# Half-folded mixer rows for batch 0, and a third head pair of q on the hardware queue

## The chip, the cores and the metric

The kernel runs on one core of a Trainium2 chip. The metric is the device time of one execution in microseconds (us). A core has five engines that work side by side: TensorE (PE, matmuls; PEld is its weight load), VectorE (DVE), ScalarE (ACT), GpSimd (POOL) and SyncE (SP, which here only starts DMAs). TensorE writes its results to PSUM, a memory of eight banks; VectorE and ScalarE copy them out.

## The reference

Eight batches; attention over keys and values that are averaged over groups of 8 tokens, then a mixer over tokens and over channels:

```
k_p = k.reshape(B, H, Sp, 8, D).mean(axis=3)      # B=8, H=8, S=576, D=64, Sp=72
v_p = v.reshape(B, H, Sp, 8, D).mean(axis=3)
x   = softmax(q @ k_p^T / sqrt(D)) @ v_p          # then heads side by side: (B, 576, 512)
u   = x + (relu(x^T @ w_tok1) @ w_tok2)^T         # w_tok1 576 x 256, w_tok2 256 x 576
out = u + relu(u @ w_ch1) @ w_ch2                 # w_ch1 512 x 1536, w_ch2 1536 x 512
```

Inputs and outputs are fp32; the kernel multiplies in bf16.

## The kernel before

**Units and batches.** The mixer's channel part is done in nine units (`unit_steps`, L546): unit n takes the first 512 tokens of batch n, and a last unit takes the 64 remaining tokens of all eight batches. A unit first makes the 1536 hidden channels as 12 blocks m of 128: four matmuls of 512 columns each over the transposed rows `uT` (L553), and a relu on ScalarE into `GT` (L557). Then it makes the output, 12 matmuls for each block c of 128 tokens (L575), and `store` adds u on VectorE (L561) and writes it out by SP. The generator yields after every two matmuls of 512 columns, so a full unit has 48 steps.

**The order of work.** Every engine has one queue of instructions, and its order is written out by hand in strings. `HEAD` (L597) lists the steps of batch 0 before unit 0. `FIRST`, `SECOND`, `THIRD`, `FOURTH` and `LATER` (L600 to L617) give, for units 0, 1, 2, 3 and all later ones, what is put in at which of the unit's steps: a plain name is a step of batch n+1, `>` one of batch n+2, `<` one of batch n itself, and `lk2` starts the load of k for batch n+2.

**Names of steps.** `K0 K1 V0 V1` average half the heads of k or v on GpSimd (`pool8`, L141; three additions), `k0 v0 v1` the same on VectorE, `kpool vpool` on TensorE (L224). `kpT` (L193) transposes the averaged k; it needs both of `K0` and `K1`. `Q0` to `Q3` transpose q on VectorE (L246). `s0 s1 s2` make scores and their exp on ScalarE (L258 and L263, L276 and L297). `av0` to `av4` (L378) multiply by v and divide; `at0 at1` (L429) are the first token matmul with its relu into `AT`; `u0` to `u4` (L440, L449) the second, with x added; `t0` to `t4` (L458) transpose u into `uT`. From batch 3 on this goes through DRAM instead (`M`, `T`).

**Batch 0 in the head.** `c0 c1` cast the first two head pairs of q, which SP loads as fp32 into `qf` (L648); the other two pairs come through GpSimd's queue with a cast in the DMA (`load_q`, L102). On GpSimd's queue they stand after k and ahead of v. `kp0` to `kp3` average k of one pair on TensorE (L202) with a cast into `kpz` by VectorE, by ScalarE for kp1 (L205); `kt` transposes (L213) and VectorE copies to `kT` (L216). `q0` to `q3` transpose q (L237). `e`, `o` (L313) and `z` (L333) are scores with exp. `w30A` is `half_av` (L341) of token block 3 and head half 0: matmuls (L350), a reciprocal, and the division on VectorE (D) or as four scaled copies on ScalarE (A); a trailing t or p names another PSUM pool. `g`, `h` (L410) are parts of the token matmul, half 0 and half 1, a third digit choosing one m. `d8` are matmuls that only keep TensorE busy.

**The folded rows.** For batch 0, `uT` isn't transposed from u. `X0` to `X3` (L491) put the transposed x into four PSUM banks, one for each part kk, by multiplying with the identity, and `A0 A1` (L499) add the second token matmul to the same banks, transposed by exchanging its operands. Four casts (L502), two on VectorE, two on ScalarE, write `uT`. u itself is still needed for the store, and is made in unit 0 (`<u0` to `<u3`).

**Buffers.** PSUM's eight banks are three of `ps_one` (one bank each, taken in turn), two of `ps_two` (two banks each) and one of `ps_tr`. A step that takes a bank waits until the reader of the use before is done.

Of the kernel before, what the change touches and what calls it, by code (L numbers as in the profile page):

```python
# [8 lines left out]
FP32 = mybir.dt.float32  # L9
# [12 lines left out]
def kernel(  # L22
# [14 lines left out]
    nc = tc.nc  # L37
# [30 lines left out]
    w_ch1 = singles.tile([P, 4, DC], BF16)  # L68
    w_ch2 = singles.tile([P, NM, DM], BF16)
    f2 = singles.tile([P, 2, S], BF16)  # L70
    qf = singles.tile([P, 2, BR * D], FP32)
    kpz = singles.tile([SP, H, 4, D], BF16)
    uT_tails = singles.tile([P, 4, 4 * P], BF16)
    u_tails = singles.tile([P, 4, DM], BF16)
# [23 lines left out]
    def load_q(b):  # L98
        qb = loaded[b, "q"] = raw.tile([P, HP, BR * D + D], BF16, name="qb")
        if b == 0:  # L100
            nc.vector.memset(qb[:, :, BR * D:], 0.0)
            nc.gpsimd.dma_start(out=qb[:, 2:HP, 0:BR * D], in_=q_pairs(2, HP))  # L102
        else:
            nc.gpsimd.dma_start(out=quarters(qb), in_=q[b].rearrange("(g l) (j n) d -> (l j) g (n d)", l=4, n=2 * BR))  # L104

# [48 lines left out]
    def batch_steps(b):  # L154
# [297 lines left out]
        def uT(c):  # L452
            def go():
                src = st["u"][:, c, :] if c < 4 else u_tails[:, b // 2, :]
                dst, o = (late("uT"), c * P) if c < 4 else (uT_tails, b // 2 * P)
                ps = ps_tr.tile([P, 4, P], BF16, name="pt")
                for kk in range(4):
                    nc.tensor.transpose(out=ps[:, kk, :], in_=parts(src)[:, kk], identity=ident)  # L458
                nc.vector.tensor_copy(out=dst[:, :, o:o + P], in_=ps)
            return go  # L460

        def spill(i):
# [18 lines left out]
                                    in_=st["v"][:, 4 * c:4 * c + 4, :].rearrange("t a (f k) -> t a k f", k=4))  # L481
            return go

        def uT_x(kk, c0, c1):

            def go():
                if c0 == 0:
                    st["uT_ps", kk] = (ps_one.tile([P, 512], FP32, name="p1") if kk < 3 else
                                       ps_two.tile([P, 2, 512], FP32, name="p2")[:, 0])
                for c in range(c0, c1):  # L490
                    nc.tensor.matmul(out=st["uT_ps", kk][:, c * P:(c + 1) * P],  # L491
                                     lhsT=parts(st["x"][:, c, :])[:, kk], rhs=ident, start=(c == 0), stop=False)
            return go

        def uT_a(m):
            def go():
                for kk in range(4):
                    ps = st["uT_ps", kk]
                    nc.tensor.matmul(out=ps, lhsT=parts(st["AT"][:, m, :])[:, kk], rhs=w_tok2[:, m, 0:512],  # L499
                                     start=False, stop=(m == 1))  # L500
                    if m == 1:
                        (nc.scalar.copy if kk % 2 else nc.vector.tensor_copy)(out=late("uT")[:, kk, :], in_=ps)  # L502
            return go

        name = {"kpT": kpT}
# [24 lines left out]
        for c in range(5):  # L530
            for a in range(2):
                for e in "DA":
                    for bank in ("", "t", "p"):
                        name[f"w{c}{a}{e}{bank}"] = half_av(c, a, e, bank)
        for kk in range(4):
            name[f"X{kk}"] = uT_x(kk, 0, 4)
        name["A0"], name["A1"] = uT_a(0), uT_a(1)
        name["Xa"], name["Xb"] = uT_x(0, 0, 2), uT_x(0, 2, 4)
        for i in range(3):
            name[f"M{2 * i}"] = spill(i)  # L540
        name["M"] = quads
# [4 lines left out]
    def unit_steps(n, st):  # L546

        GT = gtp.tile([P, NM, 4 * P], BF16, name="GT")
        uT = uT_tails if n == B else st["uT"]
        for m in range(NM):  # L550
            ps = ps_one.tile([P, 512], FP32, name="p1")
            for kk in range(4):
                nc.tensor.matmul(out=ps, lhsT=w_ch1[:, kk, m * P:(m + 1) * P], rhs=uT[:, kk, :],  # L553
                                 start=(kk == 0), stop=(kk == 3))
                if kk == 1:
                    yield
            nc.scalar.activation(out=GT[:, m, :], in_=ps, func=AF.Relu)  # L557
            yield
        def store(c, ps):
            o_sb = outp.tile([P, DM], FP32, name="o")  # L560
            nc.vector.tensor_tensor(out=o_sb, in0=ps, in1=(u_tails if n == B else st["u"])[:, c, :], op=ALU.add)  # L561
            for half in range(2):
                b, r = (2 * c + half, 8) if n == B else (n, 2 * c + half)
                nc.sync.dma_start(out=out[b].rearrange("(p r) n -> p r n", r=BR)[:, r, :],
                                  in_=o_sb[half * BP:(half + 1) * BP, :])

        runs = [(c, 0, NM) for c in range(3 if n == B else 4)]
        if n == 0:
            runs[0:2] = [(c, m, m + 4) for m in (0, 4, 8) for c in range(2)]
        pss = {}  # L570
        for c, m0, m1 in runs:
            if m0 == 0:
                pss[c] = ps_one.tile([P, 512], FP32, name="p1")
            for m in range(m0, m1):
                nc.tensor.matmul(out=pss[c], lhsT=GT[:, m, c * P:(c + 1) * P], rhs=w_ch2[:, m, :],  # L575
                                 start=(m == 0), stop=(m == NM - 1))
                if m == NM - 1:
                    store(c, pss[c])
                if m % 2 == 1:
                    yield  # L580
        if n < B:
            return
        for a in range(2):
            cols = slice(a * 256, (a + 1) * 256)
            ps = ps_one.tile([P, 512], FP32, name="p1")
            for m in range(NM):
                nc.tensor.matmul(out=ps[:, 0:256], lhsT=GT[:, m, 3 * P:4 * P], rhs=w_ch2[:, m, cols],  # L587
                                 start=(m == 0), stop=(m == NM - 1))
            o_sb = outp.tile([P, DM], FP32, name="o")[:, 0:256]
            nc.vector.tensor_tensor(out=o_sb, in0=ps[:, 0:256], in1=u_tails[:, 3, cols], op=ALU.add)  # L590
            for half in range(2):
                (nc.scalar if half else nc.sync).dma_start(
                    out=out[6 + half].rearrange("(p r) n -> p r n", r=BR)[:, 8, cols],
                    in_=o_sb[half * BP:(half + 1) * BP, :])


    HEAD = """c0 c1 d8 q0 d1 q1 d5 kp0 kp1 kt0 kp2 e0 o0 kt1 kp3 kt2 o1 q3 q2 e1 kt3 vpool0 z2 z0 w30A w10Dt  # L597
              w00D z1 w20Dt vpool1 w40Dt g21 w11D w21Dp g20 g11 g40 g31 g10 w01D g30 g00 w31D h1 w41Dp g41 h0 h2
              h3 g01 X1 h4 X2 Xa X3 Xb A0 A1"""
    FIRST = {0: "<u1 <u3", 1: "<u2 <u0 k0 lv2", 3: "Q0 Q1", 4: "lk3", 6: "lq3 Q2", 7: "Q3", 10: "kpool1 v0",  # L600
             11: "lv3", 12: "kpT", 14: "s0", 15: "v1", 19: "s1", 25: "s2", 26: "av0", 27: "av1", 29: ">K1 av2",
             30: "av4", 31: "av3", 33: "at1", 34: "at0", 35: ">K0", 36: ">V1 u0", 37: "u2 u1", 38: ">V0", 39: "t0",
             41: "t1 u4 u3", 42: "t2", 44: "t3", 46: "t4"}
    SECOND = {0: "lq3 Q0 kpT", 1: "Q1 lv3 Q2", 2: ">K1", 3: "s0", 4: ">V0", 6: "Q3", 7: ">K0 lk3", 8: "s1 >V1",
              13: "s2", 16: "av0 av1", 19: "av2", 20: "av3", 22: "av4", 23: "at0", 24: "at1 >Q0", 26: "u0", 27: "u1",
              29: "t0", 31: "u2 t1", 32: "u3 t2", 34: "t3", 35: "lq4", 36: ">kpT >Q1", 37: ">Q2 lv4", 39: ">s0",
              43: ">Q3", 44: ">s1", 47: "lk4"}
    THIRD = {0: "av1 >V0", 1: ">K1", 3: ">K0", 4: "av0", 6: "av3", 7: "av2", 9: "av4", 10: ">Q0 >V1 at0", 11: "at1",
             14: "u0", 15: "u2 u1", 17: "u3 M0 M2", 18: "u4 M4", 19: ">Q1", 24: "M", 26: ">Q3 >kpT", 28: ">s0 lq4",
             29: ">Q2", 32: ">s1 lk4", 33: "T0", 34: "lv4", 36: "T1 T2", 38: ">av0", 39: ">av2", 41: ">av1 T3",  # L610
             45: ">av3", 46: ">av4", 47: "T4"}
    FOURTH = {1: ">V0 M4 u4 at0 at1", 2: ">K0", 3: "u0", 4: "u1", 5: ">K1", 7: "u2", 9: "u3 M0", 10: "M2 >V1",
              11: "M", 14: ">Q1", 20: "lq4 >kpT", 21: "lv4", 22: ">Q0", 23: ">Q2", 24: "T0 lk4", 26: ">s0", 28: ">Q3",
              29: "T1", 32: "T2 >s1", 35: "T3", 36: "T4", 39: ">av0", 41: ">av1", 43: ">av2", 46: ">av4 >av3"}
    LATER = {0: ">V0", 1: "at1 at0", 2: ">V1", 3: "u0 >K0 u1", 5: "u2 u4", 9: "M4 >K1", 11: "M0 u3", 12: "M2",
             14: "M", 18: ">Q1 >kpT", 19: ">Q0", 21: ">s0", 24: ">Q3", 27: ">Q2", 28: ">s1", 29: "T0 T1", 30: "T2",
             34: "T3", 35: ">av1", 38: ">av0", 39: "T4", 41: ">av2", 46: ">av4 >av3"}  # L617
    warm = singles.tile([P, 512], BF16)

    def head(s):  # L620
# [23 lines left out]
    with tc.manual_schedule(engines={PE, POOLE, DVE, ACT, SYNC}):  # L644
        batches = [batch_steps(b) for b in range(B)]
        nc.vector.memset(warm, 0.0)
        for a in range(2):
            nc.sync.dma_start(out=qf[:, a:a + 1, :], in_=q_pairs(a, a + 1))  # L648
        load("k", 0)
        make_identity(nc, ident)  # L650
# [53 lines left out]
```

The softmax here doesn't subtract the row's maximum and nothing guards it: scores larger than these inputs give would overflow.

## Time and profile before

| what | us |
|---|---|
| median of 8 runs | 273.78 (273.32 to 274.53) |
| the profiled execution | 273.53 |
| its span, first to last instruction | 271.8 |
| idle of TensorE's weight loads for k, at 6.92 | 0.88 |
| the same for v, at 12.05 | 0.79 |
| first matmul of unit 0 | at 22.76 |
| first hidden matmul of unit 1 | at 55.96 |

Durations of single operations before:

| operation | ns |
|---|---|
| relu into GT, ScalarE, 128x512 (L557) | 598 |
| cast into uT, 128x512: VectorE, ScalarE (L502) | 685, 588 |
| u plus x, VectorE, 128x512 (L449) | 688 |
| fp32 q cast, 128x576: ScalarE, VectorE (L627) | 672, 460 |
| averaging half of k or v on GpSimd (L144, L145, L148 or L150) | 2120, 1264, about 720 |

The page of the profile lists groups of instructions by line; an engine's idle time ahead of a group is given with what ended it. The answers in order of time give start, duration, engine, line and operation. Matmuls overlap: the distance between two starts is the cost in a stream[...].

### The profile page before, as it was taken

The page shows a single profiled execution, that of the slowest core. Times are in us where ns is not written, and L with a number is a line of the kernel's source. Part 1 is how long each engine was busy: PE and PEld are TensorE (multiplying, and loading weights), DVE is VectorE, ACT ScalarE, POOL GpSimd, SP SyncE. Part 2 cuts the span into 40 slices and gives each one's busy share as a digit, 9 for nine tenths or more (in the row PEclk, how much of TensorE's full clock was granted, in tenths as well). Part 3 has the DMA queues.
Part 4 walks back from the last instruction along what each step waited for, and adds up shares of the span by engine and source line. Part 5 has one row for each costly group of instructions (what it writes and reads, how often), then busy time and mean ns, then how long its engine had stood idle before and what let it go on. Part 6 is the DMA issues. An engine that isn't in the chain of part 4 may idle for free.

```text
span 271.8 us, 4534 instructions
## 1 busy us (share of the span) xinstructions
PE 264.4 (97%) x1812; PEld 129.3 (48%) x1812; DVE 142.0 (52%) x279; ACT 110.9 (41%) x192; POOL 130.5 (48%) x119
## 2 busy tenths in 40 slices
PE   7899999999999999999999999999999999999994
PEld 3774444444454544544444445544454444444443
DVE  4587777862684754776366537743773161022022
ACT  2443780058206536325732483158304503603700
POOL 8694222999995994999199999300000000000000
PEclk9999999999999999999999999999999999999999
DMA  8999999995548957994399372224133544024024
GB/s 170 184 202 208 203 205 206 222 200 93 88 72 154 212 107 154 150 221 125 80 165 212 99 136 59 69 67 118 42 78 92 119 75 102 1 61 94 2 52 103
DMA packets 40149, 33.99 MB, mean 125 GB/s; under 512 B 16960, under 2 KB 33600, under 8 KB 40128
## 3 DMA queue, kind: packets, MB, share of 16 engines
q0 software_dynamic: 18672, 17.64, 41.0%
q1 hardware_dynamic: 21296, 15.93, 23.4%
q8 instruction: 14, 0.23, 0.4%
q10 hardware_dynamic: 160, 0.13, 0.2%
q14 instruction: 7, 0.06, 0.1%
HBM read 38.86 MB, written 12.45 MB: 189 GB/s over the span
## 4 chain that ended last, share of the span: by engine, by line
PE 89%; ACT 3%; DMA 2%; DVE 2%; POOL 1%; issue 1%; POOLq 0%
PE p L553 33%; PE p L575 32%; PE p L429 6%; PE p L440 5%; PE p L378 3%; DMA vr<-in_v_dram 2%; PE p L276 2%; ACT ex L263 1%; ACT GT L557 1%; PE p L224 1%; PE p L587 1%; PE pt L276 1%; PE p L446 1%; PE pt L458 1%; ACT ex L297 1%
## 5 line engine op out<-in xcount | busy, mean ns | idle before, releaser
L557 ACT ACTIVATE GT<-p 128x512 bf16<-128x512 f32 x108 | 63.9, 598 | 90.5 <-PE p L553 90.2
L575 PE MATMUL p<-w_ch,GT 128*128 128x512 bf16 x420 | 100.1, 379 | 0.0
L553 PE MATMUL p<-uT,w_ch 128*128 128x512 bf16 x384 | 91.8, 379 | 0.1
L553 PEld LDWEIGHTS <-w_ch 128*128 128x128 bf16 x432 | 40.5, 98 | 48.2 <-issue 3.1
L575 PEld LDWEIGHTS <-GT 128*128 128x128 bf16 x420 | 38.4, 98 | 40.4
L561 DVE TENSOR_TENSOR o<-p,u 128x512 f32<-128x512 f32 x32 | 21.9, 685 | 52.0 <-PE p L575 52.0
L449 DVE TENSOR_TENSOR u<-p,x 128x512 bf16<-128x512 f32 x32 | 21.5, 688 | 18.8 <-PE p L440 18.4
L145 POOL TENSOR_TENSOR t<-t 72x512 f32<-72x512 f32 x24 | 30.3, 1264 | 1.9
L144 POOL TENSOR_TENSOR t<-kr 72x1024 f32<-72x1024 bf16 x12 | 25.4, 2120 | 7.9 <-DMA kr<-in_k_dram 7.1
L144 POOL TENSOR_TENSOR t<-vr 72x1024 f32<-72x1024 bf16 x12 | 25.5, 2126 | 0.7
L297 ACT ACTIVATE ex<-p 72x1024 bf16<-72x1024 f32 x20 | 19.3, 1015 | 8.9 <-PE p L276 8.9
L246 DVE STREAM_TRANSPOSE qD<-qb 128x576 bf16<-128x576 bf16 x28 | 20.6, 795 | 0.4 <-DMA qb<-in_q_dram 0.4
L396 DVE TENSOR_TENSOR x<-p,den 128x512 bf16<-128x512 f32 x28 | 19.4, 692 | 1.0
L440 PE MATMUL p<-AT,w_tok 128*128 128x512 bf16 x64 | 18.2, 379 | 0.2 <-ACT GT L557 0.2
L378 PEld LDWEIGHTS <-ex 72*128 72x128 bf16 x280 | 13.1, 98 | 8.0 <-DVE x L396 0.6
L480 DVE STREAM_TRANSPOSE uT<-v 128x512 bf16<-128x512 bf16 x20 | 12.9, 686 | 6.0 <-DMA v<-mem 5.9
L429 PE MATMUL p<-x,w_tok 128*128 128x512 bf16 x56 | 14.5, 379 | 0.0
L378 PE MATMUL p<-vp,ex 72*128 72x65 bf16 x280 | 14.3, 194 | 0.2 <-ACT ex L263 0.2
L390 DVE RECIPROCAL den<-p 128x8 f32<-128x8 f32 (+1 forms) x35 | 7.0, 200 | 12.5 <-PE p L378 12.2
L104 POOL DMA_DIRECT2D qb<-in_q_dram x7 | 5.2, 738 | 16.8 <-DVE qD L246 13.0
L429 PEld LDWEIGHTS <-w_tok 128*128 128x128 bf16 x70 | 6.8, 98 | 8.4 <-issue 0.3
L86 POOL DMA_DIRECT2D vr<-in_v_dram x10 | 7.7, 774 | 6.1 <-DMA kr<-in_k_dram 3.1
(109 smaller groups left out, 218.4 us busy)
## 6 DMA issues: line engine op xcount, KB each, us to landing
out_dram<-o SPq DMA_DIRECT2D x70, 128.0 KB, 2.4
kr<-in_k_dram POOLq DMA_DIRECT2D x7, 576.0 KB, 12.9
qb<-in_q_dram POOLq DMA_DIRECT2D x7, 576.0 KB, 6.7
vr<-in_v_dram POOLq DMA_DIRECT2D x7, 576.0 KB, 14.9
w_ch<-in_moe_w_ch_dram POOLq DMA_DIRECT2D x6, 512.0 KB, 13.4
mem<-u SPq DMA_DIRECT2D x10, 256.0 KB, 2.1
v<-mem SPq DMA_DIRECT2D x12, 160.0 KB, 3.6
v<-mem SPq DMA_DIRECT2D x8, 128.0 KB, 3.3
```

Source lines behind the costliest of these rows:

```text
L144: eng.tensor_tensor(out=t4[:, 0:n], in0=t[:, hs, 0:4], in1=t[:, hs, 4:8], op=ALU.add)
L145: eng.tensor_tensor(out=t4[:, 0:n, 0:2], in0=t4[:, 0:n, 0:2], in1=t4[:, 0:n, 2:4], op=ALU.add)
L246: nc.vector.transpose(out=late("qD")[:, g, db].rearrange("m (r j u) -> m u r j", u=2, r=BR), in_=st["qraw"][:, g].rearrange("m (u r d) -> ...
L297: nc.scalar.activation(out=exv[:, a, :, 0:8 * BP], in_=main[a][0:SP], func=AF.Exp, scale=scale)
L378: nc.tensor.matmul(out=halves[h // 4][:, (h % 4) * (D + 1):(h % 4 + 1) * (D + 1)], lhsT=st["ex"][:, h * S + n0:h * S + n0 + P], rhs=st["vp ...
L429: nc.tensor.matmul(out=ps, lhsT=w_tok1[:, c if c < 4 else 4 + par, m * P:(m + 1) * P], rhs=st["x"][:, c, :] if c < 4 else st["xt"], start= ...
L440: nc.tensor.matmul(out=ps, lhsT=w_tok2[:, m, c * P:(c + 1) * P], rhs=st["AT"][:, m, :], start=(m == 0), stop=(m == 1))
L449: nc.vector.tensor_tensor(out=dst, in0=ps, in1=x, op=ALU.add)
L553: nc.tensor.matmul(out=ps, lhsT=w_ch1[:, kk, m * P:(m + 1) * P], rhs=uT[:, kk, :], start=(kk == 0), stop=(kk == 3))
L557: nc.scalar.activation(out=GT[:, m, :], in_=ps, func=AF.Relu)
L561: nc.vector.tensor_tensor(out=o_sb, in0=ps, in1=(u_tails if n == B else st["u"])[:, c, :], op=ALU.add)
L575: nc.tensor.matmul(out=pss[c], lhsT=GT[:, m, c * P:(c + 1) * P], rhs=w_ch2[:, m, :], start=(m == 0), stop=(m == NM - 1))
```

## The change

For batch 0, only the first 256 tokens of `uT` are folded. `X0` and `X1` now take two parts kk each, with two token blocks; `A0` and `A1` multiply by 256 columns. Two casts instead of four remain, of the same size. The other 256 tokens are transposed from u, as in later batches: `u2` and `u3` move to the end of the head, `t2` and `t3` into unit 0's first steps, with the copy on ScalarE and `t3` in a `ps_one` bank. So that unit 0 can begin with the first 256 tokens, its first four hidden blocks are made in two halves of 256 tokens (`hidden`); the number of steps stays the same.

The third head pair of q moves from GpSimd's queue to SP's, as fp32, with the cast `c2` on ScalarE. All six order strings differ.

```diff
-    qf = singles.tile([P, 2, BR * D], FP32)
+    qf = singles.tile([P, 3, BR * D], FP32)
...
-            nc.gpsimd.dma_start(out=qb[:, 2:HP, 0:BR * D], in_=q_pairs(2, HP))
+            nc.gpsimd.dma_start(out=qb[:, 3:HP, 0:BR * D], in_=q_pairs(3, HP))
...
-                ps = ps_tr.tile([P, 4, P], BF16, name="pt")
+                odd = first and c % 2
+                ps = (ps_one if odd else ps_tr).tile([P, 4, P], BF16, name="p1" if odd else "pt")
                 for kk in range(4):
                     nc.tensor.transpose(out=ps[:, kk, :], in_=parts(src)[:, kk], identity=ident)
-                nc.vector.tensor_copy(out=dst[:, :, o:o + P], in_=ps)
+                (nc.scalar.copy if first else nc.vector.tensor_copy)(out=dst[:, :, o:o + P], in_=ps)
...
+        def uT_x(j):
+            def go():
+                ps = st["uT_ps", j] = ps_one.tile([P, 2, 256], FP32, name="p1")
+                for i in range(2):
+                    for c in range(2):
+                        nc.tensor.matmul(out=ps[:, i, c * P:(c + 1) * P], lhsT=parts(st["x"][:, c, :])[:, 2 * j + i],
+                                         rhs=ident, start=(i == c == 0), stop=False)
             return go
 
         def uT_a(m):
             def go():
-                for kk in range(4):
-                    ps = st["uT_ps", kk]
-                    nc.tensor.matmul(out=ps, lhsT=parts(st["AT"][:, m, :])[:, kk], rhs=w_tok2[:, m, 0:512],
-                                     start=False, stop=(m == 1))
+                for j in range(2):
+                    ps = st["uT_ps", j]
+                    for i in range(2):
+                        nc.tensor.matmul(out=ps[:, i, :], lhsT=parts(st["AT"][:, m, :])[:, 2 * j + i],
+                                         rhs=w_tok2[:, m, 0:256], start=False, stop=(m == 1 and i == 1))
                     if m == 1:
-                        (nc.scalar.copy if kk % 2 else nc.vector.tensor_copy)(out=late("uT")[:, kk, :], in_=ps)
+                        (nc.scalar.copy if j else nc.vector.tensor_copy)(out=late("uT")[:, 2 * j:2 * j + 2, 0:256], in_=ps)
...
-        for m in range(NM):
+        def hidden(m, n0, n):
             ps = ps_one.tile([P, 512], FP32, name="p1")
             for kk in range(4):
-                nc.tensor.matmul(out=ps, lhsT=w_ch1[:, kk, m * P:(m + 1) * P], rhs=uT[:, kk, :],
+                nc.tensor.matmul(out=ps[:, 0:n], lhsT=w_ch1[:, kk, m * P:(m + 1) * P], rhs=uT[:, kk, n0:n0 + n],
                                  start=(kk == 0), stop=(kk == 3))
-                if kk == 1:
+                if kk == 1 and n == 512:
                     yield
-            nc.scalar.activation(out=GT[:, m, :], in_=ps, func=AF.Relu)
+            nc.scalar.activation(out=GT[:, m, n0:n0 + n], in_=ps[:, 0:n], func=AF.Relu)
             yield
+
+        early = 4 if n == 0 else 0
+        for half in range(2):
+            for m in range(early):
+                yield from hidden(m, half * 256, 256)
+        for m in range(early, NM):
+            yield from hidden(m, 0, 512)
...
-    HEAD = """c0 c1 d8 q0 d1 q1 d5 kp0 kp1 kt0 kp2 e0 o0 kt1 kp3 kt2 o1 q3 q2 e1 kt3 vpool0 z2 z0 w30A w10Dt
-              w00D z1 w20Dt vpool1 w40Dt g21 w11D w21Dp g20 g11 g40 g31 g10 w01D g30 g00 w31D h1 w41Dp g41 h0 h2
-              h3 g01 X1 h4 X2 Xa X3 Xb A0 A1"""
-    FIRST = {0: "<u1 <u3", 1: "<u2 <u0 k0 lv2", 3: "Q0 Q1", 4: "lk3", 6: "lq3 Q2", 7: "Q3", 10: "kpool1 v0",
-             11: "lv3", 12: "kpT", 14: "s0", 15: "v1", 19: "s1", 25: "s2", 26: "av0", 27: "av1", 29: ">K1 av2",
...
-    SECOND = {0: "lq3 Q0 kpT", 1: "Q1 lv3 Q2", 2: ">K1", 3: "s0", 4: ">V0", 6: "Q3", 7: ">K0 lk3", 8: "s1 >V1",
...
-              29: "t0", 31: "u2 t1", 32: "u3 t2", 34: "t3", 35: "lq4", 36: ">kpT >Q1", 37: ">Q2 lv4", 39: ">s0",
...
-    THIRD = {0: "av1 >V0", 1: ">K1", 3: ">K0", 4: "av0", 6: "av3", 7: "av2", 9: "av4", 10: ">Q0 >V1 at0", 11: "at1",
...
-             24: "M", 26: ">Q3 >kpT", 28: ">s0 lq4",
-             29: ">Q2", 32: ">s1 lk4", 33: "T0", 34: "lv4", 36: "T1 T2", 38: ">av0", 39: ">av2", 41: ">av1 T3",
+    HEAD = """c0 c1 c2 d8 q0 d1 q1 d5 kp0 kt0 kp1 kp2 o0 kp3 e0 kt1 kt2 o1 q3 q2 e1 kt3 vpool0 z2 z0 w30A w10Dt z1
+              w00D w20Dt vpool1 w40Dt g21 w21A w11D g40 w01D g11 g10 g31 g00 w31D g20 g30 g41 h1 w41D h2 h0 h3
+              X0 h4 g01 X1 A0 A1 u2 u3"""
+    FIRST = {0: "<t2", 1: "<t3", 2: "<u0", 3: "<u1 k0", 5: "Q0 Q1", 6: "Q2 lk3 lv2", 7: "Q3", 8: "lq3", 10: "kpool1",
+             11: "lv3", 13: "kpT v0", 14: "v1", 15: "s0", 20: "s1", 25: "s2", 26: "av0", 27: "av1", 28: "av2",
+             29: ">K1", 30: "av4", 31: "av3", 33: "at1", 34: "at0", 35: ">K0", 36: "u0", 37: "u1", 38: ">V0 u3",
+             39: "t0 u2", 41: "t1 u4", 42: "t2", 44: "t3", 45: ">V1", 46: "t4"}
+    SECOND = {0: "kpT lq3 lv3 Q0", 1: "Q1 Q2", 3: "lk3 s0", 4: "Q3", 5: ">K1 >V0", 7: ">K0", 8: "s1 >V1", 13: "s2",
...
+              30: "u2 t1", 31: "u3", 32: "t2", 34: ">Q1 t3", 35: "lq4", 36: "lv4 >kpT", 39: ">Q2 >s0", 43: ">Q3",
...
+    THIRD = {0: ">V0 >K1", 1: ">V1 av1", 3: ">K0", 4: "av0", 6: "av3", 7: "av2", 9: "av4", 10: ">Q0 at0", 11: "at1",
...
+             28: ">s0 lq4", 30: "lk4", 31: ">Q2", 33: "lv4", 35: ">s1", 36: "T2 T0", 39: "T1", 40: ">av0", 41: ">av2",
...
-        for a in range(2):
+        for a in range(3):
             nc.sync.dma_start(out=qf[:, a:a + 1, :], in_=q_pairs(a, a + 1))
```

`FOURTH` and `LATER` move single steps by a few places.

## The prediction

> **What bounds the kernel now.** I read the page first (busy shares, slices, chain), then TensorE's busy time by stage, then the order of time in the first 28 us, and last the places further on where the new order of steps could make something late.
>
> ```profile
> span 271.8 us, 4534 instructions
> PE 264.4 (97%) x1812; PEld 129.3 (48%) x1812; DVE 142.0 (52%) x279; ACT 110.9 (41%) x192; POOL 130.5 (48%) x119
> PE 89%; ACT 3%; DMA 2%; DVE 2%; POOL 1%; issue 1%; POOLq 0%
> ```
>
> TensorE holds 89% of the chain. The chain in order of time has 48 second-layer matmuls in 10.36 us, so one of 512 columns takes 0.216 us; four single L410 matmuls of 256 columns start at 18.65, 18.76, 18.87 and 18.97, so 0.108 us; twelve transposing ones of 128 columns last 0.83 us with a last one of 0.22, so 0.056 us. Busy time by stage, columns PE, PEld, DVE, ACT, POOL, clock, DMA share, GB/s:
>
> ```profile
> 7.00:11.40 4.40, 4.32 (x66) 3.70 (x66) 2.75 (x8) 2.23 (x5) 2.44 (x5) 1.00 1.17 175
> 11.40:12.00 0.60, 0.00 (x0) 0.00 (x0) 0.45 (x2) 0.59 (x1) 0.35 (x1) 1.00 1.25 206
> 22.80:28.40 5.60, 5.42 (x25) 2.34 (x25) 4.09 (x11) 2.29 (x5) 0.94 (x2) 1.00 1.21 208
> 140.00:168.00 28.00, 28.00 (x201) 13.17 (x200) 16.09 (x31) 12.53 (x22) 26.43 (x21) 1.00 0.66 141
> ```
>
> From unit 3 on TensorE is full, so reordered steps can give nothing there; only the head and units 0 to 2 have room. The DMA engines are busy (over 1.1) from 4 us. The 0.6 us without TensorE before 12.0 is the head's wait for v. In order of time:
>
> ```profile
> 6.92 0.93 PEld L202 LDWEIGHTS <-ident 72*72 72x72 bf16 x16 [0.88 <-DMA kr<-in_k_dram]
> 7.60 0.42 DVE L205 CAST kpz<-p 72x256 bf16<-72x256 f32 x1 [1.61 <-PE p L202]
> 12.05 0.80 PEld L224 LDWEIGHTS <-ident 72*72 72x72 bf16 x8 [0.79 <-DMA vr<-in_v_dram]
> 20.05 0.60 ACT L420 ACTIVATE AT<-pt 128x512 bf16<-128x512 f32 x1 [3.57 <-PE pt L410]
> 20.71 1.92 PE L499 MATMUL p<-w_tok,AT 128*128 128x512 bf16 x8
> 22.01 1.29 DVE L502 CAST uT<-p 128x512 bf16<-128x512 f32 x2 [1.16 <-PE p L499]
> 22.76 0.59 PE L553 MATMUL p<-uT,w_ch 128*128 128x512 bf16 x2
> 25.33 0.59 PE L440 MATMUL p<-AT,w_tok 128*128 128x512 bf16 x2 [0.18 <-ACT GT L557]
> ```
>
> So the head has two DMA waits (k at 6.92, v at 12.05), and its end runs through relu, the folded rows, their casts and unit 0's first matmul. For unit 2:
>
> ```profile
> 99.97 0.72 POOL L148 TENSOR_TENSOR kp<-t 72x256 bf16<-72x256 f32 x1
> 104.76 0.29 PE L193 MATMUL pt<-ident,kp 72*128 72x72 bf16 x4
> 108.73 0.18 PE L276 MATMUL pt<-qD,kD 32*72 32x64 bf16 x1 [0.26 <-ACT ex L299]
> ```
>
> POOL's pooled k of batch 4 is ready at 100.7, 4 us ahead of its transposes; the second score step there waits for ScalarE's exp.
>
> [...] the share is already 1.20 between 4 and 7 us, so a further transfer there must displace one. [...]
>
> **Part 1, the folded rows.** Removed: 8 of the 16 transposing X matmuls (8 x 0.056 = 0.45 us) and half of the columns of the 8 A matmuls (8 x 0.108 = 0.86). Added: t2 and t3, 8 transposes (0.45). The first four m of unit 0 become 32 matmuls of 0.108 in place of 16 of 0.216, no change. Net TensorE work: -0.86 us.
>
> Stalls there before, from the starts above and of the neighbours, against 0.216 a matmul: 0.08 ahead of A0, 0.30 ahead of 22.76 (the casts), 0.08 and 0.34 around u2 and u0 (their buffers): 0.8 us. After, counted from the start T of h4 (19.75 before):
> - relu on ScalarE starts at T+0.30 and lets A0 start at T+0.95 as now, but g01 and X1 fill only until T+0.54: 0.41 idle. Before, 12 X matmuls filled this.
> - A0 and A1 end at T+1.81. The cast of j=0 on VectorE runs to T+2.5 (685 ns), of j=1 on ScalarE to T+2.6 (588). u2 covers 0.43 of that; u3 needs the first cast's bank (ps_one has three): 0.26 idle.
> - From unit 0's first matmul at about T+2.9, ScalarE has the relus of 385 ns and the copies of t2 and t3 (about 0.57 each, between the 588 of a cast and the 400 of the 288-column copy plus 224 columns) on one bank rotation: u0 waits about 0.25, m3 0.1, and after u1's add once more 0.1.
>
> Sum of stalls after: 1.1 us; difference +0.3. The same work (u0 to u3 and m0 to m3) then ends at T+8.2 where it ended at T+8.6: gain about 0.4, between 0 (if each copy is late by another 0.2) and 0.8 (if none is).
>
> **Part 2, the third q pair.** Its 288 KB leave POOL's queue, ahead of v, for SP's. By the trace's records of single DMA packets, an fp32 q transfer of one pair (128 packets) on SP's queue lasts about 0.73 us (175 packets per us), on POOL's 0.88 (145 per us). Thus v lands 0.15 earlier, but the transfer now runs from 3.65 us, ahead of or among k's packets: k lands later, by up to 0.73. The cast c2 (672 ns like c0) lies in ScalarE's idle time before 8 us and costs nothing. The head's order also puts kt0 straight after kp0: transposes of kpz wait for its cast, 7.60 to 8.02 before, so idle 0.67 in place of 0.23, and o1 waits some 0.4 for kt1's copy on VectorE. From kp0 to vpool0 the matmuls take 3.9 us (32 pooling ones of 0.056 are 1.8, 16 transposes of some 0.035 are 0.55, ten of q 0.56, eight scores of 256 or 320 columns 0.98); with 0.35 of waits they ended at about 11.2 before, 0.8 ahead of v. With 1.1 us of waits and a start at 7.65, vpool0 comes at 12.65 in place of 12.08: +0.55. If k is not delayed, 6.92 + 5.0 = 11.92, about where v then bounds it: -0.1. I take +0.5. w21's four multiplies on ScalarE relieve VectorE, but w31 then waits for that bank (about 0.4 on TensorE); by my count h4 is at the same distance from vpool0 (7.67 us) as before, so nothing there.
>
> **Part 3, the orders of the later steps.**
> - Unit 2: POOL's order becomes V0 K1 V1 K0. Each takes 4.34 us from 87.74, so K0 ends at 105.05, while kpT keeps its step 26 (104.76 before): +0.3 to +0.4. s1 moves from step 32 to 35, 1.3 us later, when the exps are done: its excess wait of 0.33 goes.
> - Unit 1: u3 one step before t2 takes away most of a 0.19 wait at 78.14. k of batch 4 is issued before the pooling, delaying K0 to about 78.3; kpT is at 80.31, hidden.
> - Unit 0: loads of v2 come after k3 on POOL and DMA, so V0 of batch 2 may wait 0.4 us at 54.4; av0 needs it at about 65, hidden.
>
> Together -0.2, between -0.5 and +0.5.
>
> **Sum.** -0.4 + 0.5 - 0.2 = -0.1 us on the profiled execution's 273.53 (span 271.8 and 1.7 around it), which lies 0.25 below the median of 273.78. I forecast no change, 273.7 us, its own range 273.2 to 274.3.
>
> **Rivals.**
> - *K late, slower.* One mechanism: kp0 waits for k behind the third q pair, so that the TensorE chain of the head, not v, sets vpool0. It decides from k being late by more than about 0.25 us beyond what part 1 gives back; at the full 0.73, with part 1's gain at 0.1, and unit 2's K0 at its 0.4: 0.6 - 0.1 + 0.3 = +0.8, so 274.6. For it: share of 1.2 between 4 and 7 us. Against it: 0.75 us of slack before 12.05.
> - *v still bounds, faster.* k's packets keep their place, vpool0 comes 0.1 earlier, stalls in unit 0 are smaller: -0.1 - 0.6 - 0.2 = -0.9, so 272.9. For it: the page counts 0.86 us of real work less on the bounding engine. Against it: the order kp0 kt0.
> - *The saving goes to unit 0's scores.* ScalarE carries about 1.8 us more (two copies of 0.57[...]) and is full between 33 and 38 us (4.86 of 5); if its backlog lasted until then, +0.5. Against it: it idles 3.7 us among the first five relus. 274.3.
>
> **How the numbers follow.** No change 0.33; K late 0.31; unit 0's scores, half of it past the bound, 0.08; v still bounds 0.28. A measurement here can tell about 0.2%, 0.55 us, from no change. Faster 0.29, same 0.34, slower 0.37. The range from 272.7 to 274.9 leaves out the far ends of both.
>
> **What would show it.** Right: kp0 0.5 to 0.7 later, vpool0 at about 12.6, unit 0's first matmul at T+2.9, some 1.1 us of gaps from h4 to m4, kpT of batch 4 waiting on POOL at about 105, s1 without a wait. Wrong: kp0 still at 6.9 (then faster), or gaps above 1.5 us between the head's end and m4, or POOL late for unit 1's kpT (then slower by more than 0.8).

## The result and the profile after

The changed kernel is slower. Median of 11 runs 278.40 us (274.66 to 281.68), beside 274.02 for the kernel before (32 runs, 273.1 to 276.6); ratio 1.0115, 95% interval 1.0085 to 1.0144. The ratio leaves out runs more than 1.5% above the fastest of their kernel, four of the 11; the plain quotient of the medians is 1.016. The profiled execution took 277.90 us against 273.53, 4.37 more, and its span is 4.3 longer.

The page of the changed kernel: the span, the busy shares, the granted clock of TensorE in 40 slices of 6.9 us, and the chain by engine:

```profile
span 276.1 us, 4576 instructions
PE 267.6 (97%) x1828; PEld 133.9 (49%) x1828; DVE 141.5 (51%) x277; ACT 113.7 (41%) x202; POOL 130.3 (47%) x119
PEclk9779999999999999999999999999999999999999
PE 79%; POOL 7%; DMA 5%; DVE 3%; ACT 2%; issue 2%; SPq 0%; POOLq 0%; DVEq 0%
```

TensorE's busy time rose by 3.2 us although its columns fell by 0.86 us' worth of work. The clock row gives the main reason: slices 1 and 2, from 6.9 to 20.7 us, stand at 7, where the kernel before has 9 everywhere. TensorE's share of the chain fell from 89% to 79%, and POOL and DMA came in. Where the clock fell, in busy times by stage (columns as before: PE, PEld, DVE, ACT, POOL, clock, DMA share, GB/s):

```profile
4.00:7.00 3.00, 3.00 (x16) 1.70 (x15) 1.44 (x3) 0.42 (x1) 2.98 (x5) 1.00 1.09 190
7.00:9.00 2.00, 0.85 (x4) 0.17 (x2) 0.00 (x0) 0.15 (x1) 0.54 (x1) 1.00 1.18 183
9.00:10.00 1.00, 0.64 (x8) 0.48 (x8) 0.29 (x1) 0.53 (x1) 0.70 (x2) 1.00 1.19 182
10.00:17.00 7.00, 6.66 (x60) 5.89 (x61) 2.82 (x9) 2.51 (x5) 4.37 (x7) 0.54 1.28 199
```

From 7 to 9 us TensorE is busy for 0.85 of 2.00: it has run out of filling matmuls. Another 0.36 us is missing from 9 to 10. Then, from 10 to 17, it runs at a mean clock of 0.54. Where the fall lies, shorter stretches of the same profile show:

```profile
10.30:10.50 0.20, 0.20 (x8) 0.20 (x7) 0.00 (x0) 0.00 (x0) 0.00 (x0) 1.00 1.17 183
10.60:10.80 0.20, 0.20 (x6) 0.20 (x4) 0.20 (x1) 0.00 (x0) 0.00 (x0) 0.50 1.26 196
```

The clock column misses one thing. Up to 6.9 us the filling matmuls of 512 columns start 0.427 us apart, which is half rate, although the column reads 1.00; from 7.25 on they start 0.217 apart. In the profile of the kernel before full rate comes at 4.5 us. This isn't the change's doing: in before_warm below, whose queues start as before, the filling matmul at 5.12 still takes 0.63 us, like the one at 5.11 here; before, the one at 4.79 takes 0.38. It is why the filling matmuls last until 7.85 here, and until 6.5 before. In order of time:

```profile
8.85 0.67 ACT L634 CAST qb<-qf 128x576 bf16<-128x576 f32 x1 [4.43 <-DMA qf<-in_q_dram]
9.03 0.64 PE L202 MATMUL p<-kr,ident 72*72 72x128 bf16 x8 [1.18 <-DMA kr<-in_k_dram]
...
16.76 1.34 PE L224 MATMUL p<-vr,ident 72*72 72x256 bf16 x8
...
25.41 1.06 PE L499 MATMUL p<-w_tok,AT 128*128 128x256 bf16 x8 [0.25 <-ACT AT L420]
...
27.47 0.60 PE L551 MATMUL p<-uT,w_ch 128*128 128x256 bf16 x4
...
108.95 0.30 PE L193 MATMUL pt<-ident,kp 72*128 72x72 bf16 x4 [0.42 <-POOL kp L148]
```

The averaging of k (L202) begins at 9.03, not at 6.92. The averaging of v (L224, `vpool0`) begins at 16.76, not at 12.08, and no DMA stands beside it: v is long there, TensorE itself is late. From these starts, and those of the units' first hidden matmuls, the 4.3 us come out as follows:

| stretch | before | after | difference |
|---|---|---|---|
| start to `vpool0` | 12.08 | 16.76 | +4.68 |
| `vpool0` to h4 | 7.67 | 7.69 | +0.02 |
| h4 to unit 1 (unit 0 within it) | 36.21 | 35.44 | -0.77 |
| unit 1, unit 2 | 61.29 | 61.33 | +0.04 |
| unit 3 | 27.69 | 28.09 | +0.40 |
| unit 4 and the rest | | | about 0 |

So, in this pair of profiles, all that is lost is lost before `vpool0`. The stretch with the folded rows gave 0.77 us, unit 3 takes half of it back.

### The profile page after: what moved, and what is told of

It is laid out like the page before. It is cut to its first block, busy times and chain, and to the rows that moved or that the text cites. A ratio compares the mean times of both kernels' runs of the same rounds, so it can differ in the third digit from the quotient of the medians.

```text
span 276.1 us, 4576 instructions
## 1 busy us (share of the span) xinstructions
PE 267.6 (97%) x1828; PEld 133.9 (49%) x1828; DVE 141.5 (51%) x277; ACT 113.7 (41%) x202; POOL 130.3 (47%) x119
## 4 chain that ended last, share of the span: by engine, by line
PE 79%; POOL 7%; DMA 5%; DVE 3%; ACT 2%; issue 2%; SPq 0%; POOLq 0%; DVEq 0%
PE p L581 30%; PE p L551 26%; PE p L429 5%; PE p L440 4%; POOL t L144 3%; PE p L378 3%; DMA kr<-in_k_dram 3%; POOL t L145 2%; DMA mem<-u 2%; ACT ex L263 1%; PE p L276 1%; DMA v<-mem 1%; PE p L202 1%; PE p L224 1%; PE p L593 1%
## 5 line engine op out<-in xcount | busy, mean ns | idle before, releaser
L555 ACT ACTIVATE GT<-p 128x512 bf16<-128x512 f32 (+1 forms) x112 | 64.7, 583 | 88.2 <-PE p L551 87.6
L551 PE MATMUL p<-uT,w_ch 128*128 128x512 bf16 (+1 forms) x400 | 92.5, 371 | 0.0
L551 PEld LDWEIGHTS <-w_ch 128*128 128x128 bf16 x448 | 42.0, 98 | 46.9 <-issue 2.9
L86 POOL DMA_DIRECT2D kr<-in_k_dram x10 | 7.9, 786 | 10.8 <-PE p L224 9.1
```

Of the source, the lines that this page charges most:

```text
L551: nc.tensor.matmul(out=ps[:, 0:n], lhsT=w_ch1[:, kk, m * P:(m + 1) * P], rhs=uT[:, kk, n0:n0 + n], start=(kk == 0), stop=(kk == 3))
L555: nc.scalar.activation(out=GT[:, m, n0:n0 + n], in_=ps[:, 0:n], func=AF.Relu)
```

## The experiments

My theory after the result: the third q transfer delays k, TensorE then idles, its clock drops, and the head runs slowly up to `vpool0`; the rest of the change is worth little. The rivals: the new order of the head does it, or the new orders of the units. Each run has its own runs of the kernel before, whose median was 274.04 to 274.23 us.

**q_back**: the changed kernel, with the third pair back on GpSimd's queue.

```diff
-    qf = singles.tile([P, 3, BR * D], FP32)
+    qf = singles.tile([P, 2, BR * D], FP32)
...
-            nc.gpsimd.dma_start(out=qb[:, 3:HP, 0:BR * D], in_=q_pairs(3, HP))
+            nc.gpsimd.dma_start(out=qb[:, 2:HP, 0:BR * D], in_=q_pairs(2, HP))
...
-    HEAD = """c0 c1 c2 d8 ...
+    HEAD = """c0 c1 d8 ...
...
-        for a in range(3):
+        for a in range(2):
```

> The changed kernel with the third q pair back on GpSimd's queue (no c2), all else as changed. Theory A (the third pair on SP's queue delays k to about 9 us, and TensorE, idle until then, drops to half its clock for much of the head): kp0 back at 6.9 us, no half clock after 10 us, 273.5 to 274.3 us. Rival B (the half-folded rows and unit 0 in token halves cost it, by bank waits and small matmuls): stays above 276 us.

274.07 us (273.03 to 274.69), ratio 0.9993 (0.9980 to 1.0006). The whole loss is gone, and the mean clock is 0.999. But k's averaging doesn't come back to 6.9, which I had expected:

```profile
8.46 0.64 PE L202 MATMUL p<-kr,ident 72*72 72x128 bf16 x8 [1.11 <-DMA kr<-in_k_dram]
9.61 0.30 PE L213 MATMUL p<-ident,kpz 72*128 72x72 bf16 x4 [0.52 <-DVE kpz L205]
```

With the pair back on GpSimd's queue k is still late in this execution, and `vpool0` starts at 13.55. TensorE waits 1.11 and 0.52 us, nearly as in the changed kernel (1.18 and 0.52), and keeps its clock: 1.00 from 10 to 17 us. So k's landing varies from execution to execution without the transfer too, and here waits of this size didn't cost the clock.

**q_alone**: the kernel before with this part only (the same lines the other way, and `c2` in `HEAD`).

> The kernel before with only the third q pair moved to SP's queue and c2. Theory A: kp0 at 8.5 to 9.1 us, the head's end 2.5 to 5 us later than before, a wide scatter of times, 276 to 279 us. Rival B: the transfer is hidden, at most 274.6 us.

278.40 us (275.30 to 279.21), ratio 1.0146 (1.0110 to 1.0183): the part alone gives the whole loss. k's averaging starts at 10.20, later than I expected, `vpool0` at 17.13. Busy times by stage of q_alone:

```profile
7.00:10.00 3.00, 0.00 (x0) 0.00 (x0) 0.00 (x0) 0.33 (x1) 0.00 (x1) 1.00 1.14 198
10.00:14.00 4.00, 3.73 (x39) 3.22 (x40) 1.15 (x3) 1.38 (x4) 2.58 (x5) 0.66 1.24 202
14.00:18.00 4.00, 4.00 (x35) 3.59 (x34) 2.23 (x6) 1.81 (x4) 3.58 (x5) 0.50 1.28 177
```

Three microseconds without a matmul, and then half clock, as in the changed kernel.

**fold_alone**: the kernel before with the folded rows, the token halves and the new `FIRST`; `HEAD` keeps its order but for its end.

```diff
-              h3 g01 X1 h4 X2 Xa X3 Xb A0 A1"""
+              h3 g01 X0 h4 X1 A0 A1 u2 u3"""
```

> The kernel before with only the half-folded rows, u2 and u3 in the head, unit 0 in halves and its new order; q and the orders of units 1 and later as before. Theory A with the prediction's working: 0.2 to 0.8 us faster than before, 273.2 to 273.8 us. Rival B: 276 us or more.

273.31 us (272.62 to 273.94), ratio 0.9970 (0.9958 to 0.9983). This part is a gain of 0.8 us by the ratio.

**orders_alone**: the kernel before with `SECOND` to `LATER` exchanged.

> The kernel before with only the orders of unit 1 and all later units exchanged. Read from the two profiles: unit 2 waits 0.4 to 0.6 us for K0 at the transposes of k and loses the wait ahead of its second scores, unit 3 gains a wait of 0.3 us: in all 0.2 to 0.6 us slower than before, 274.2 to 274.6 us. Rival C (these orders only hurt behind a late head): no difference within 0.2 us.

274.16 us (273.58 to 274.98), ratio 1.0002 (0.9991 to 1.0013): no difference, where I had expected 0.2 to 0.6 us. `kpT` in unit 2 has a gap of 0.61 us at 105.30, `s1` has none; unit 1 is 0.07 shorter, unit 2 0.13 longer. The rival of the later orders falls.

The next ones ask how much of the loss is the clock, and why k is late.

**q_warm**: q_alone with 18 filling matmuls in place of 5, so that TensorE works until k is there.

```diff
-    HEAD = """c0 c1 c2 d8 q0 d1 q1 d5 kp0 ...
+    HEAD = """c0 c1 c2 d8 q0 d1 q1 d18 kp0 ...
```

> The kernel before with the third q pair on SP's queue and c2, as q_alone, but 18 instead of 5 filling matmuls between q1 and kp0, so that TensorE has work until about 9.2 us. If the half clock is most of the price (A1): no half clock after 10 us, mean clock 0.997 or more, 275 to 276.3 us. If the late k itself is (A2): unchanged at 277.8 to 278.8 us.

275.82 us (275.51 to 276.88), ratio 1.0059 (1.0037 to 1.0082). Busy times by stage of q_warm:

```profile
7.00:10.00 3.00, 3.00 (x16) 1.34 (x15) 0.00 (x0) 0.49 (x1) 0.43 (x1) 1.00 1.15 180
10.00:14.00 4.00, 3.93 (x58) 3.38 (x57) 1.90 (x6) 1.80 (x5) 2.14 (x5) 1.00 1.24 198
```

k's averaging starts as late as in q_alone (10.42 against 10.20; the filling matmuls end just there), yet from 10 to 14 us TensorE gets through 58 matmuls, not 39, and the clock stays at 1.00. `vpool0` comes at 14.74 instead of 17.13, and the kernel is 2.6 us faster for useless matmuls. So of q_alone's 4.2 us about 2.6 are the half clock, and 1.7 (275.82 against 274.13) the late start.

**q_gpsimd**: q_alone, its third fp32 transfer on GpSimd's queue, ahead of k: the same bytes ahead of k, one queue less.

```diff
-            nc.sync.dma_start(out=qf[:, a:a + 1, :], in_=q_pairs(a, a + 1))
+            (nc.gpsimd if a == 2 else nc.sync).dma_start(out=qf[:, a:a + 1, :], in_=q_pairs(a, a + 1))
```

> The kernel before with the third q pair as fp32 and c2, but on GpSimd's own queue ahead of k, the same bytes and the same place ahead of k. If two queues at once slow each other (M): k is later only by the transfer's 0.7 us, kp0 at 7.5 to 8.2 us, 273.9 to 275 us. If it is the bytes ahead of k (N): kp0 at 8.5 us or later and 276 us or more.

273.96 us (273.62 to 275.65), ratio 0.9992 (0.9981 to 1.0003); k's averaging at 8.44, the clock 1.0. The time is the one forecast for M; k's start lies between the two forecasts, and no later than in q_back (8.46), where no third transfer stands ahead of k. So the bytes ahead of k alone don't make the loss. What the transfers move from 4 to 7 us is in the DMA view by queue (packets, MB, and the time their packets took, as a share of 16 engines' time; q0 is GpSimd's queue, q1 SP's). Of the kernel before:

```profile
q0 software_dynamic: 649, 0.56, 119.8%
q1 hardware_dynamic: 3, 0.00, 0.1%
```

Of the changed kernel:

```profile
q0 software_dynamic: 362, 0.30, 80.7%
q1 hardware_dynamic: 134, 0.27, 28.2%
```

Of q_alone:

```profile
q0 software_dynamic: 307, 0.24, 75.2%
q1 hardware_dynamic: 111, 0.23, 34.0%
```

Of q_back, where the third pair isn't on SP's queue:

```profile
q0 software_dynamic: 417, 0.34, 103.7%
q1 hardware_dynamic: 4, 0.00, 0.4%
```

Together 0.56, 0.57, 0.47 and 0.34 MB. At the rate of the kernel before, about 0.19 MB/us (0.56 MB in 3 us), the 0.27 MB on SP's queue are 1.4 us. This is an estimate, for the rate isn't constant: q_back's queue moves no more than 0.34 MB although it has the engines nearly to itself. On k's own queue the transfer had partly passed before 4 us: GpSimd's queue has 0.11 MB from 3 to 4 us in q_gpsimd and 0.04 before, while SP's has 0.30 and 0.32 in the same microsecond. The median landing of k's loads after their issue is 4.8 us before, 5.9 in q_gpsimd, 6.9 in the changed kernel and 8.6 in q_alone. Each is one execution, and these scatter: 4.8 to 6.5 us in the profiles of the eight kernels that leave the third pair behind k (4.8 before is the earliest, 6.5 is q_back), 6.9 to 8.6 in the four that have it on SP's queue from the start. The two groups don't overlap; their medians, 5.75 and 7.7, are 2 us apart. With q's packets on SP's queue, GpSimd's, which carries k, moved 0.30 and 0.24 MB in these three microseconds, against 0.56 before; but q_back's moved 0.34 without them. Why q_alone moves 0.09 MB less in all, and why the same bytes on k's own queue delay k less, isn't shown.

**q_late**: q_alone, its third transfer held back by a one-element copy on VectorE until the first part of k is there, and `c2` behind it.

```diff
-    HEAD = """c0 c1 c2 d8 q0 d1 q1 d5 kp0 ...
+    HEAD = """c0 c1 d8 q0 d1 q1 y c2 d5 kp0 ...
+        elif s == "y":
+            nc.vector.tensor_copy(out=qf[0:1, 2, 0:1], in_=loaded[0, "k"][0:1, 0, 0, 0:1])
+            nc.sync.dma_start(out=qf[:, 2:3, :], in_=q_pairs(2, 3))
```

> The kernel before with the third q pair on SP's queue, but started only when the first part of k has landed (a one-element copy on VectorE holds it). If sharing the engines with k is what hurts: kp0 at 6.9 to 7.6 us as before, no half clock, 273.6 to 275 us, v perhaps up to 1 us later. If a second queue hurts wherever it runs: 276 us or more.

280.22 us (279.18 to 284.36), ratio 1.0201 (1.0169 to 1.0234), a miss. k was no longer late (averaging at 7.52), but another wait came in. The order of time of q_late:

```profile
7.18 0.33 SPq L627 DMA_DIRECT2D qf<-in_q_dram  x1
...
13.27 0.67 ACT L630 CAST qb<-qf 128x576 bf16<-128x576 f32 x1 [8.90 <-DMA qf<-in_q_dram]
...
14.27 0.42 PE L213 MATMUL p<-ident,kpz 72*128 72x72 bf16 x4 [4.21 <-ACT kpz L205]
```

The transfer, issued at 7.18, landed after 6.0 us; this run's first two q transfers took 2.9 and 4.4. From 7 to 8 us only GpSimd's queue has packets (0.19 MB, 118.0% in the view by queue), SP's none. `c2` held ScalarE until 13.27, and the cast of kp1 stood behind it, so TensorE idled 4.2 us in another place and the clock fell again (mean 0.987). The question it was made for, whether k in time is enough, it can't answer.

**after_warm** and **before_warm**: the changed kernel and the kernel before, each with `d18` for `d5`. The first takes the low clock away from the change; the second makes the head late without any q transfer.

```diff
-    HEAD = """... q1 d5 kp0 ...
+    HEAD = """... q1 d18 kp0 ...
```

> The changed kernel with 18 instead of 5 filling matmuls between q1 and kp0, nothing else. If the half clock behind the late k is most of its price (A1): clock 0.997 or more, 274.8 to 275.8 us, narrow scatter. If it is the late k alone (A2): 277.5 us or more, as the changed kernel.

> The kernel before with 18 instead of 5 filling matmuls: TensorE then reaches kp0 at about 9.1 to 9.5 us at full clock although k landed at about 7, so the head is late without any change of the DMAs. By the head's slack of 0.8 us ahead of v, the price of that lateness alone should be 1.2 to 1.8 us: 275.2 to 276 us. If lateness alone costs nothing: at most 274.4 us.

after_warm: 275.08 us (274.70 to 275.87), ratio 1.0044 (1.0030 to 1.0058). before_warm: 275.71 us (275.20 to 276.29), ratio 1.0059 (1.0047 to 1.0072). Busy times by stage of after_warm:

```profile
10.00:14.00 4.00, 3.40 (x54) 3.17 (x55) 2.20 (x7) 2.21 (x4) 2.81 (x5) 1.00 1.24 199
14.00:18.00 4.00, 3.84 (x58) 3.52 (x56) 3.00 (x11) 3.19 (x9) 3.00 (x4) 1.00 1.31 201
```

The clock is 1.00, and k's averaging is where it was (9.21 against 9.03, now straight behind the filling matmuls), so 3.3 of the change's 4.4 us by medians (278.40 to 275.08) were the clock. What remains, 1.0 us, is near the 0.8 that the rival *K late, slower* had for k 0.73 late. before_warm puts a price on lateness alone: k's averaging at 10.00, `vpool0` at 14.32, and 1.7 us more than before, as much as q_warm has with the q transfer in it. So once the start is that late, the transfer itself costs nothing more that can be told. At full clock the distance from the averaging to `vpool0` is 4.32 us in the old order of the head (q_warm and before_warm) and 5.07 in the new (after_warm); in the changed kernel it was 7.73, so half clock cost 2.66 us there.

**head_order**: fold_alone with the changed kernel's `HEAD`, without `c2`.

> fold_alone with the changed kernel's order of the head (kt0 straight after kp0, w21 on ScalarE, and so on), q as before. By the prediction's working, kt0's wait grows by 0.45 us and o1 waits 0.4: with the slack ahead of v 0 to 0.6 us slower than fold_alone, 273.3 to 273.9 us. Rival: the head's order makes the changed kernel's loss, 275 us or more.

273.78 us (272.69 to 275.72), ratio 0.9995 (0.9983 to 1.0007), by the medians 0.5 more than fold_alone. That is within what I expected, but the two intervals of the ratio meet at 0.9983. In its profile `vpool0` starts 5.09 us after k's averaging, at 13.02 instead of fold_alone's 12.22; unit 0 is longer too, by 0.85, most of it a wait for batch 1's k. So the 0.5 isn't shown to be the head's order alone.

**fold_best**: fold_alone with the new `SECOND` and `THIRD`, except that in `THIRD` V1 of batch 4 goes back behind K0, which lets K0 end earlier.

```diff
-    THIRD = {0: ">V0 >K1", 1: ">V1 av1", 3: ">K0", ... 10: ">Q0 at0",
+    THIRD = {0: ">V0 >K1", 1: "av1", 3: ">K0", ... 10: ">Q0 >V1 at0",
```

> fold_alone with the new orders of units 1 and 2, except that V1 stays behind K0 in unit 2, so that kpT finds K0 ready. Expected from the profiles: unit 2 loses the wait ahead of its second scores (0.33 us) without the 0.59 us at kpT, 0.2 to 0.5 us faster than fold_alone, 272.7 to 273.2 us. Rival: reorders in units 1 and 2 don't show, as fold_alone within 0.15 us.

272.56 us (272.25 to 273.21), ratio 0.9938 (0.9917 to 0.9958). In order of time, fold_best's unit 2:

```profile
99.19 0.72 POOL L148 TENSOR_TENSOR kp<-t 72x256 bf16<-72x256 f32 x1
...
103.72 0.29 PE L193 MATMUL pt<-ident,kp 72*128 72x72 bf16 x4
```

K0 is ready at 99.9, four microseconds ahead of its transposes, and no wait stands beside them. Unit 2 takes 29.76 us, 0.49 less than before. This version beats both kernels; that it also beats fold_alone isn't clear, as the two intervals meet at 0.9958.

**fold_best2**: fold_best with the changed kernel's head from `vpool0` on, where `w21` is divided by ScalarE.

> fold_best with the changed kernel's order of the head from vpool0 on (w21 on ScalarE), and the order of the kernel before ahead of vpool0. In the kernels with the new head h4 comes 7.38 us after vpool0, in fold_alone 7.66: 0.2 to 0.4 us faster than fold_best, 272.2 to 272.4 us. Rival: the new head's tail gives nothing, within 0.15 us of fold_best.

272.78 us (271.79 to 274.24), ratio 0.9951 (0.9937 to 0.9965). The distance from `vpool0` to h4 shrank to 7.39 us from 7.66, but the intervals of the two overlap: no gain that can be told.

## Why the prediction was wrong

I forecast no change, 273.7, with k's delay as the main risk; the median came out 4.7 us above. The likeliest rival on the slower side, *K late*, had the sign, with +0.8 where +4.4 was measured.

**Part 2, k's delay: the term that failed first.** It says "k lands later, by up to 0.73". k's averaging came 2.11 us later in the pair of profiles, 6.92 and 9.03; by the medians of all the profiles k landed about 2 us later. The 0.73 was the time of a q transfer beside little else, 128 packets at 175 per us, thus 0.40 MB/us. The transfer moved into a stage where the engines move about 0.19 MB/us, which stood in the profile's stages as 175 to 208 GB/s: at that rate, an estimate, 0.27 MB ahead of k are 1.4 us. Of the remaining 0.7 a part can be scatter, since 4.8 us is the earliest landing of its group, and a part may lie in the use of two queues, as q_gpsimd pays nothing; the runs don't settle how much. The forecast's conclusion that a further transfer "must displace one" agrees with the changed kernel's queues (0.30 MB on GpSimd's from 4 to 7 us, 0.56 before, with the sum at 0.57 and 0.56) and with k's later landing in all four kernels; the price was too low.

**The sum: a clock taken for constant.** Every price in the forecast (0.216, 0.108, 0.056 us a matmul) is one at full clock, and no step asked what TensorE does while k is late. It ran out of filling matmuls at 7.85, idled 1.18 us, and from about 10.6 to 17.4 matmuls of 128 columns started 0.107 apart, not 0.056. That is 2.66 us, the largest single term. q_warm and after_warm, whose filling matmuls last until k is there, kept the clock at 1.00 from 10 to 14 us. But the waits alone don't tell when it falls: in the changed kernel the fall at 10.55 came after 1.18 us of one wait and 0.52 of another, while q_back, with 1.11 and 0.52, kept its clock, and so did one of the 11 runs of the changed kernel (0.998). What tips it isn't shown. The row of clocks in the profile of before, 9 in every slice, gave no sign of it; the wait for k at 6.92 was a hint.

The loss up to `vpool0`, 4.68, can be split into k late, less v's slack, new order, half clock. Before, v came 5.16 us after k's averaging started, where 4.32 would have done: slack 0.84. So 2.11 - 0.84 + 0.75 + 2.66 = 4.68. The split adds up by construction; its middle terms rest on the distances in q_warm, before_warm and after_warm.

**Part 2, the rest, was right.** The cast `c2` ran at 8.85 instead of before 8, since its transfer landed 7.2 us after its issue, but nothing waited for it. The new order's waits: 5.0 us from kp0 to `vpool0` forecast, 5.07 and 5.09 measured; what they cost, up to 0.5 us by head_order, lies near the noise. The same distance from `vpool0` to h4: 7.67 forecast, 7.69 measured. This hides two things that cancel: q_warm and after_warm have 7.66 and 7.38, so the new order gave 0.28 (0.11 of it only because g01 now stands behind h4), and the changed kernel gave it back: it still had half clock from 16.76 to 17.4, which costs half of that time, about 0.32.

**Part 1 had the mechanism, and half of the size.** -0.4 forecast (0 to -0.8), -0.77 measured; the work from h4 to m3 ended at T+8.0, forecast T+8.2, before T+8.6. Its steps: the relu of 256 columns took 0.38 to 0.43 us (forecast 0.385; ScalarE's 588 ns at 512 columns and 400 at 288 in the trace of before are 0.84 ns a column, thus, as an estimate, 598 - 256 x 0.84 = 383 ns), the copies 0.58 and 0.60 (0.57), the gaps ahead of A0 and u3, by the starts, 0.41 and 0.30 (0.41 and 0.26; the 0.25 beside the line at 25.41 counts from a modelled end), unit 0's first matmul at T+3.0 (T+2.9). The gap that I had put before u0, 0.25, was 0.08. About 0.2 of the gain came later in unit 0, which I hadn't counted. fold_alone's 0.8 by ratio agrees.

**Part 3 was right in three places and missed a fourth.** `kpT` waits about 0.59 for K0 (forecast 0.3 to 0.4), `s1` no longer waits, unit 1 gains 0.07. Missed: unit 3 takes 0.40 longer. There `s1` waits 0.46 us for VectorE, whose Q3 stands behind T0, and T0 waits for rows that go through DRAM; SP's wait for them grew to 3.8 us from 1.8. The new order of unit 3 issues M two steps later and leaves T0 ahead of Q3. But that isn't enough: with orders_alone the wait stayed at 1.8 and unit 3 at its old length, with q_back it was 4.0 and unit 3 28.35, and after_warm, which has every part of the change, has 1.8 and 27.70 again. What decides stayed open.

**The rivals.** *K late, slower* named the place and the side, and its 274.6 is near after_warm's 275.08, and near the one run of the changed kernel whose mean clock was 0.998 (274.66). It lacked the clock. *v still bounds* and *The saving goes to unit 0's scores* didn't happen: no DMA stands at 16.76, and unit 0 was shorter, although its eight relus of 256 columns (392 ns on the mean) took 0.75 us more than four of 512 (596 ns).

## What to carry to other kernels

When a transfer is moved ahead of one that the bounding engine waits for, price the delay by the bytes at the rate measured in the stage that it moves into (0.19 MB/us here), not by the rate of the transfer beside little else (0.40), and look at more than one profile: here the same loads landed up to 1.7 us apart without any transfer moved. Then ask what the bounding engine does meanwhile, and read its clock by stage: here TensorE's wait of 1.18 us for k was followed by 6.8 us at half clock, which cost 2.66 us up to `vpool0`, more than the wait itself. A few useless matmuls until the data are there took that price away here (278.40 to 275.08), but the late data's own price, 1.0 us, stayed.

## What the runs showed of the hardware that I had not expected

- Half clock for 6.8 us (10.55 to 17.38) after waits of 1.18 and 0.52 us, though not every time (q_back). In q_alone it also lasted 6.8 us, from 11.3 to 18.1. The time of the changed kernel followed the mean clock from run to run: 274.66 us at 0.998, 276.12 and 276.47 at 0.994, 277.77 to 278.60 at 0.988, 278.34 to 280.43 at 0.981 and 0.982, 281.08 at 0.976, 281.68 at 0.966. 6.8 us at half clock take 6.8 x 0.5 / 276 = 0.012 from the mean, which agrees with the profiled run's 0.988; by the same sum, an estimate, 0.994 stands for about 3.3 us at half clock, 0.981 for 10.5, 0.976 for 13 and 0.966 for 19.
- The same fp32 transfer ahead of k cost nothing measurable on k's own queue (0.9992) and 1.46% on another queue (1.0146).
- A transfer on SP's queue, issued at 7.18 us while GpSimd's queue was busy (118.0% from 7 to 8 us), had no packets in that microsecond and took 6.0 us to land (q_late), where the first two on that queue took 2.9 and 4.4. Why is open.
